# Holding back the second MoE's weight loads until the first MoE has reached a given point

## The chip, the cores and the metric

The kernel runs on one core of a Trainium2 chip. The metric is the device time in microseconds (us) of one execution. The engines are named as in the profile: PE (matrix products), PEld (its weight loads), DVE (vector), ACT (scalar), POOL (GpSimd), SP (the queue that issues nearly all DMAs).

## The reference, cut to what matters

Three stages follow one another. The first is causal attention over 4 batches, 8 heads, 576 positions and 64 values a head, mixed with a memory term. Its output, 2304 tokens of 512 values, goes through two dense "MoE" layers:

```python
h = x @ w_in                       # first MoE: 512 -> 2048
g = h * sigmoid(h)
x = g @ w_out                      # 2048 -> 512
g = x @ w_gate                     # second MoE: 512 -> 1536, two products
out = (g * sigmoid(g) * (x @ w_val)) @ w_out
```

## The kernel before, in words

**Precision.** The MoE weights arrive as 64-bit numbers. Each 128x512 tile of them is loaded raw (512 KB), turned into fp32 by one ACT and three DVE operations (`decode`, L659 to L662), and split into a high and a low part whose sum is the fp32 number; ACT makes the high part and POOL the low one. A product then takes three passes: high times high, low times high, high times low.

**First MoE.** `moe1` walks over 32 segments (a block of 256 or 320 tokens times a quarter of the 2048 hidden columns). For each of the four hidden tiles of a segment, `s1` makes the product h (PE, L784), the activation th (ACT L791, DVE L792), its high part gh (ACT L195) and its low part gl (POOL L794). So there are 128 results gl, in a fixed order; they live in 5 buffers. The second product y (PE, L842) uses them, and its partial sums go to yp (DVE L847). The weights of this stage are decoded once, written to DRAM and reloaded from there (w<-wd, L688).

**Attention** is cut into small steps ("slots") that the program emits between the pieces of the first MoE. It uses all engines: PE for transposes and products, DVE for minima and copies, ACT for exponentials, POOL for scaling (L464).

**Weights of the second MoE.** 36 raw tiles (12 groups j, three tiles each: gate, val, out) are prepared while attention and the first MoE run. The generator `prep_w2` loads a tile with `load64` (L645 or L650), decodes it, makes for each group four sums and differences S on POOL (L918 to L921), splits everything (`halves`: ACT L195, POOL L907) and stores the parts in DRAM (L892). There are three raw buffers, and the program asks for the load two tiles ahead of the decoding. `open_w2` is the end of this: it prepares groups up to 9, then gives up the memory of attention for other pools, prepares groups 10 and 11 there, transforms the first tokens of the second MoE (`y_prep`, POOL L961), and loads the output weights (`wos`, L1008).

**Second MoE.** `up` (L1046) and `down` (L1114) run after the first MoE's last segment, in an order of PE written out by hand.

**What sets the order.** The kernel is written with a framework that allocates buffers, sets all semaphores and orders the instructions of each engine before the run: the earlier an instruction stands in the program, the higher its priority, but one whose inputs and buffers are ready by the framework's own estimate may be put ahead of earlier ones that are not. On the chip each engine, and the SP queue, then runs its list in that order.

Of the kernel before, what the change touches and what calls it, by code (L numbers as in the profile page):

```python
# [8 lines left out]
F32 = mybir.dt.float32  # L9
# [12 lines left out]
    raw=2,  # L22
# [18 lines left out]
    gl='p',  # L41
# [45 lines left out]
def kernel(  # L87
# [15 lines left out]
    nc = tc.nc  # L103
# [16 lines left out]
    def f(ap):  # L120
        return ap.bitcast(F32)
# [23 lines left out]
    cur, ph2 = {"raw": rawp}, {}  # L145
# [47 lines left out]
    def cp(e, out, in_):  # L193
        if e == "a":
            nc.scalar.copy(out, in_)  # L195
        else:
            (nc.vector if e == "v" else nc.gpsimd).tensor_copy(out, in_)
# [7 lines left out]
    def tt(e):  # L205
        return nc.vector if e == "v" else nc.gpsimd
# [431 lines left out]

    w1 = {}

    def load64(w, j, part):
        raw = cur["raw"].tile([P, 512, 2], I32, tag="raw8", name="raw8", bufs=CFG["raw8"])
        w2 = w.bitcast(I32)
        if part == 0:
            nc.sync.dma_start(  # L645
                out=raw.rearrange("p (k n) t -> p k (n t)", k=KD),
                in_=w2[:, 2 * P * j:2 * P * (j + 1)].rearrange("(k p) n -> p k n", p=P),
            )
        else:
            nc.sync.dma_start(out=raw.rearrange("p n t -> p (n t)"), in_=w2[P * j:P * j + P, :])  # L650
        return raw
# [18 lines left out]
    def raw_w1(*key):  # L670
        if key in seen:
            return None
        if key[0] == 0:
            return load64(w1_in, key[1], 0)
        raw = cur["raw"].tile([P, 512, 2], I32, tag="raw8", name="raw8", bufs=CFG["raw8"])
        _, s, e = key
        nc.sync.dma_start(
            out=raw.rearrange("p (j n) t -> p j (n t)", j=NW),
            in_=w1_out.bitcast(I32)[P * NW * s:P * NW * (s + 1), 2 * P * e:2 * P * (e + 1)].rearrange(
                "(j p) n -> p j n", p=P  # L680
            ),
        )
        return raw
# [70 lines left out]
    def moe1():  # L754
        keys = []
        for n, sg in enumerate(segs):
            if n == 0 or sg["s"] != segs[n - 1]["s"]:
                keys.append(sg["s"])
        prep1.add([(0, j) for j in SLICES[keys[0]]] + [(1, keys[0], e) for e in range(KD)])
        yield ("init", 0)  # L760
        gs = [{} for _ in segs]
        fresh = [0]

        def get_x(n):
            yield ("need", ready[segs[n]["b"], segs[n]["blk"][0] // SA])

        def s1(n, ji):
            sg = segs[n]
            s, nt = sg["s"], sg["blk"][1]
            j = SLICES[s][ji]  # L770
            xh, xl = xs[sg["b"], sg["blk"][0] // SA]
            assert n_x[sg["b"], sg["blk"][0] // SA] == NP
            if ji == 0 and sg["last_use"]:
                nk = SLICES[segs[n + 1]["s"]]
                prep1.add([(0, c) for c in nk])
                fresh[0] += len(nk)
            wh, wl = prep1.need((0, j))
            wh = wh.rearrange("p (k n) -> p k n", k=KD)
            wl = wl.rearrange("p (k n) -> p k n", k=KD)
            ps = bank("h")  # L780
            m = 0
            for w, x in ((wh, xh), (wl, xh), (wh, xl)):
                for kk in range(KD):
                    nc.tensor.matmul(  # L784
                        ps[:, :nt], w[:, kk, :], x[:, kk, :nt], start=(m == 0), stop=(m == 3 * KD - 1)
                    )
                    m += 1
            th = mt.tile([P, TM], F32, tag="th", name="th", bufs=CFG["th"])
            gh = mg.tile([P, TM], F32R, tag="gh", name="gh")
            gl = mg.tile([P, TM], F32R, tag="gl", name="gl")  # L790
            nc.scalar.activation(out=th[:, :nt], in_=ps[:, :nt], func=ACTF.Tanh, scale=0.5 / WS)  # L791
            nc.vector.scalar_tensor_tensor(th[:, :nt], th[:, :nt], 1.0, ps[:, :nt], ALU.add, ALU.mult)  # L792
            cp(CFG["gh" if n >= CFG["n0"] else "gh0"], gh[:, :nt], th[:, :nt])
            tt(CFG["gl" if n >= CFG["n0"] else "gl0"]).tensor_sub(gl[:, :nt], th[:, :nt], f(gh[:, :nt]))  # L794
            gs[n][j] = (gh, gl)
            if sg["last_use"]:
                del prep1.done[(0, j)]
                if ji >= CFG["f1"] and fresh[0] > 0:
                    prep1.step()
                    fresh[0] -= 1  # L800
            elif prep1.todo or prep1.raws:
                prep1.step()
            yield ("g", 12 * nt)

        turn = [0]

        def bank(name):

            if "g" not in ph2:
                return ps_m.tile([P, 512], F32, tag="m", name=name)  # L810
            turn[0] += 1
            i = turn[0] % 8
            if i < 3:
                return ps_m.tile([P, 512], F32, tag="m", name=name)
            return sum_bank("acbdb"[i - 3], name)

        LA = CFG["la"]
        for n, sg in enumerate(segs):
            b, blk, s = sg["b"], sg["blk"], sg["s"]
            t0, nt = blk  # L820
            yield from get_x(n)
            if sg["first"]:
                yps[b, blk] = mx.tile([P, KD, TM], F32, tag="yp", name="yp", bufs=CFG["yp"])
            yp = yps[b, blk]
            for ji in range(len(gs[n]), NW):
                yield from s1(n, ji)
                if ji == CFG["xa"] and n + 1 < len(segs) and segs[n + 1]["b"] == b:
                    yield from get_x(n + 1)
            if n + 1 == len(segs):
                stream()  # L830
            if n + 1 < len(segs) and LA:
                yield from get_x(n + 1)
                for ji in range(LA):
                    yield from s1(n + 1, ji)
            for e in range(KD):
                ps = bank("y")
                m, last = 0, 3 * len(SLICES[s]) - 1
                for wi, gi in ((0, 0), (1, 0), (0, 1)):
                    for ji, j in enumerate(SLICES[s]):
                        w, g = prep1.need((1, s, e))[wi], gs[n][j][gi]  # L840
                        c = slice(P * ji, P * ji + P)
                        nc.tensor.matmul(ps[:, :nt], w[:, c], g[:, :nt], start=(m == 0), stop=(m == last))  # L842
                        m += 1
                if sg["first"]:
                    nc.scalar.mul(yp[:, e, :nt], ps[:, :nt], 0.5 / WS**2)
                else:
                    nc.vector.scalar_tensor_tensor(  # L847
                        yp[:, e, :nt], ps[:, :nt], 0.5 / WS**2, yp[:, e, :nt], ALU.mult, ALU.add
                    )
                if sg["last"]:  # L850
                    nc.sync.dma_start(
                        out=yd[P * e:P * e + P, b * S + t0:b * S + t0 + nt], in_=yp[:, e, :nt]
                    )
                if sg["last_use"]:
                    while fresh[0] > 0:
                        prep1.step()
                        fresh[0] -= 1
                    del prep1.done[(1, s, e)]
                    prep1.add([(1, segs[n + 1]["s"], e)])
                    if e >= CFG["f2"]:  # L860
                        prep1.step()
                yield ("g", 3 * len(SLICES[s]) * nt)
# [18 lines left out]
    def prep_w2():  # L881
        todo = [(j, part) for j in range(F2) for part in range(3)]
        raws, post = [], []

        def fetch(n):
            while todo and len(raws) < n and not ("hold" in ph2 and n > 1):
                j, part = todo.pop(0)
                raws.append(load64((w2_gate, w2_val, w2_out)[part], j, part // 2))

        def flush():  # L890
            for d, t in post:
# [48 lines left out]
    def sum_bank(tag, name):  # L940
        return ph2["g"].tile([P, 512], F32, tag=tag, name=name, bufs=2 if tag == "b" else 1)
# [79 lines left out]
    def stream():  # L1021

        j = len(streamed) % F2
        ws = {}
        for t, d in enumerate(wd2[j]):
            w = wp.tile([P, 2, 512], F32, tag="w", name="w")
            w = w.rearrange("p a (b c) -> p (a b) c", c=256)
            n = d.shape[1]
            nc.sync.dma_start(out=w[:, 0:n], in_=d)
            for x in range(n // 2):  # L1030
                ws[PIECES[2 * t + x]] = (r_(w[:, 2 * x]), r_(w[:, 2 * x + 1]))
        streamed.append(ws)
# [91 lines left out]
    if True:  # L1124
# [50 lines left out]
        with tc.manual_schedule(engines={mybir.EngineType.PE}):  # L1175
            for n in range(NB2 * F2):
                i, j = divmod(n, F2)
# [56 lines left out]
```

## Time and profile before

| what | value |
|---|---|
| median of 3 runs | 1163.76 us (1161.03 to 1165.37) |
| the profiled execution | 1163.68 us |
| its span, first to last instruction | 1161.9 us |
| outside the span | 1.8 us |
| busy: PE, DVE, ACT, POOL | 95%, 56%, 45%, 48% of the span |
| granted clock of PE, mean | 0.975 |

Busy time of PE is counted from modelled ends of overlapping matmuls, so a stretch in which PE is busy throughout can still differ in the matmuls that it holds. The granted clock is a share of 2.4 GHz; the lower of the two levels is 1.2 GHz, so a mean of 0.95 in a stretch means that the lower level held for a tenth of it.

### The profile page before, as it was taken

The page shows a single profiled execution, that of the slowest core. Times are in us where ns is not written, and L with a number is a line of the kernel's source. Part 1 is how long each engine was busy: PE and PEld are TensorE (multiplying, and loading weights), DVE is VectorE, ACT ScalarE, POOL GpSimd, SP SyncE. Part 2 cuts the span into 40 slices and gives each one's busy share as a digit, 9 for nine tenths or more (in the row PEclk, how much of TensorE's full clock was granted, in tenths as well). Part 3 has the DMA queues.
Part 4 walks back from the last instruction along what each step waited for, and adds up shares of the span by engine and source line. Part 5 has one row for each costly group of instructions (what it writes and reads, how often), then busy time and mean ns, then how long its engine had stood idle before and what let it go on. Part 6 is the DMA issues. An engine that isn't in the chain of part 4 may idle for free.

```text
span 1161.9 us, 19100 instructions
## 1 busy us (share of the span) xinstructions
PE 1100.5 (95%) x6803; PEld 985.9 (85%) x6803; DVE 653.2 (56%) x1413; ACT 518.1 (45%) x1237; POOL 554.6 (48%) x566
## 2 busy tenths in 40 slices
PE   7899999988989899999999799999999999999998
PEld 5576877887879788899988699899989999999986
DVE  6996777789977888425647422433353332333320
ACT  6754766456755565634645322222242223323222
POOL 4565574569887878614536922311172122312113
PEclk9989999999989899999999799999999999999999
DMA  9975755568779685544307596666665554645511
GB/s 217 295 221 158 241 182 169 172 187 271 243 246 334 219 290 189 167 151 125 108 19 278 201 413 213 219 195 196 197 235 171 156 190 150 194 154 191 160 32 55
DMA packets 155919, 226.72 MB, mean 195 GB/s; under 512 B 75696, under 2 KB 108464, under 8 KB 155824
## 3 DMA queue, kind: packets, MB, share of 16 engines
q1 hardware_dynamic: 153648, 225.10, 60.0%
q8 instruction: 54, 0.88, 0.3%
q10 hardware_dynamic: 2176, 0.40, 0.2%
q14 instruction: 41, 0.34, 0.1%
HBM read 170.93 MB, written 54.53 MB: 194 GB/s over the span
## 4 chain that ended last, share of the span: by engine, by line
PE 69%; DVE 13%; DMA 5%; POOL 5%; issue 4%; ACT 4%; SPq 0%; ACTq 0%; POOLq 0%; DVEq 0%
PE y L842 13%; PE po L1114 12%; PE h L784 11%; PE gb L1046 9%; PE ga L1046 6%; PE U L555 3%; PE gd L1046 3%; PE gc L1046 3%; PE pst L322 2%; PE pss L422 2%; DMA wo<-wo 2%; POOL s L464 2%; DVE t L661 2%; PE pss L417 1%; DVE t L662 1%
## 5 line engine op out<-in xcount | busy, mean ns | idle before, releaser
L1100 POOL TENSOR_TENSOR pl<-r,ph 128x384 fp32r<-128x384 f32 x72 | 75.1, 1052 | 315.0 <-ACT ph L1099 254.0
L784 PE MATMUL h<-xh,w 128*128 128x320 f32 (+1 forms) x1024 | 170.7, 306 | 19.6 <-DVE th L792 15.8
L842 PE MATMUL y<-gh,w 128*128 128x320 f32 (+1 forms) x1024 | 181.5, 314 | 6.7 <-DVE th L792 4.2
L794 POOL TENSOR_TENSOR gl<-th,gh 128x256 fp32r<-128x256 f32 (+1 forms) x128 | 114.4, 897 | 141.4 <-ACT gh L195 77.6
L784 PEld LDWEIGHTS h<-xh,w 128*128 128x128 f32 x1024 | 147.2, 193 | 28.2 <-DVE th L792 16.8
L842 PEld LDWEIGHTS y<-gh,w 128*128 128x128 f32 x1024 | 152.9, 199 | 20.3 <-issue 9.3
L464 POOL TENSOR_TENSOR s<-s,r 128x128 f32<-128x128 f32 (+4 forms) x144 | 118.7, 854 | 64.6 <-DVE r L481 27.1
L1114 PE MATMUL po<-wo,ph 128*128 128x512 f32 x432 | 134.0, 395 | 3.4 <-ACT ot L1120 2.2
L1046 PE MATMUL gb<-yT,w 128*128 128x384 f32 x648 | 132.0, 338 | 0.6 <-ACT gb L1070 0.6
L1046 PEld LDWEIGHTS gb<-yT,w 128*128 128x128 f32 x648 | 116.1, 188 | 10.3 <-ACT gb L1070 1.3
L792 DVE SCALAR_TENSOR_TENSOR th<-th,h 128x256 f32<-128x256 f32 (+1 forms) x128 | 57.1, 448 | 90.6 <-ACT th L791 90.3
L1073 DVE TENSOR_TENSOR gd<-gb,e 128x384 f32<-128x384 f32 x36 | 20.4, 567 | 149.7 <-PE gb L1046 149.7
L842 PE MATMUL y<-gl,w 128*128 128x320 f32 (+1 forms) x512 | 97.7, 306 | 2.5 <-POOL gl L794 2.5
L784 PE MATMUL h<-xl,w 128*128 128x320 f32 (+1 forms) x512 | 94.5, 305 | 0.0
L195 ACT CAST gh<-th 128x256 fp32r<-128x256 f32 (+1 forms) x128 | 54.7, 431 | 86.6 <-DVE th L792 47.5
L1114 PEld LDWEIGHTS po<-wo,ph 128*128 128x128 f32 x432 | 79.1, 188 | 12.3 <-ACT ot L1120 3.1
L1046 PE MATMUL ga<-yB,w 128*128 128x384 f32 x432 | 87.2, 337 | 0.0
L1114 PE MATMUL po<-wo,pl 128*128 128x512 f32 x216 | 84.5, 399 | 0.7 <-POOL pl L1100 0.7
L431 ACT ACTIVATE s<-s,mn 128x128 f32<-128x128 f32 (+3 forms) x128 | 71.3, 558 | 29.9 <-DVE mn L427 29.1
L842 PEld LDWEIGHTS y<-gl,w 128*128 128x128 f32 x512 | 79.8, 197 | 5.6 <-POOL gl L794 3.2
L784 PEld LDWEIGHTS h<-xl,w 128*128 128x128 f32 x512 | 78.2, 196 | 3.1 <-issue 2.6
L791 ACT ACTIVATE th<-h 128x256 f32<-128x256 f32 (+1 forms) x128 | 51.6, 407 | 65.0 <-PE h L784 43.5
(141 smaller groups left out, 2060.1 us busy)
## 6 DMA issues: line engine op xcount, KB each, us to landing
w<-wg SPq DMA_DIRECT2D x108, 512.0 KB, 4.2
w<-wd SPq DMA_DIRECT2D x80, 512.0 KB, 5.1
wg<-wo SPq DMA_DIRECT2D x36, 512.0 KB, 4.6
wd<-w SPq DMA_DIRECT2D x32, 512.0 KB, 4.3
raw<-in_moe_w_out_dram SPq DMA_DIRECT2D x28, 512.0 KB, 4.4
wo<-wo SPq DMA_DIRECT2D x24, 512.0 KB, 6.7
w<-wg SPq DMA_DIRECT2D x36, 256.0 KB, 3.4
raw<-in_moe_w_in_dram SPq DMA_DIRECT2D x16, 512.0 KB, 4.9
```

The lines of the kernel that those rows point to most:

```text
L195: nc.scalar.copy(out, in_)
L431: nc.scalar.activation(out=a, in_=a, func=ACTF.Exp, scale=-1.0, bias=mn, accum_out=o["sm", sup][:, col:col + 1])
L464: nc.gpsimd.tensor_mul(a, a, r.to_broadcast([P, w]))
L555: nc.tensor.matmul(U[64 * hh:64 * hh + 64, c0:c1], row_of("v", c)[:, hh], a(hh), start=False, stop=(m == len(todo) - 1), skip_group_check= ...
L784: nc.tensor.matmul(ps[:, :nt], w[:, kk, :], x[:, kk, :nt], start=(m == 0), stop=(m == 3 * KD - 1))
L791: nc.scalar.activation(out=th[:, :nt], in_=ps[:, :nt], func=ACTF.Tanh, scale=0.5 / WS)
L792: nc.vector.scalar_tensor_tensor(th[:, :nt], th[:, :nt], 1.0, ps[:, :nt], ALU.add, ALU.mult)
L794: tt(CFG["gl" if n >= CFG["n0"] else "gl0"]).tensor_sub(gl[:, :nt], th[:, :nt], f(gh[:, :nt]))
L842: nc.tensor.matmul(ps[:, :nt], w[:, c], g[:, :nt], start=(m == 0), stop=(m == last))
L1046: nc.tensor.matmul(dst, ws[nw][wi][:, P * kk:P * kk + P], y[ny][:, yi, kk], start=(start and m == 0), stop=(stop and m == 5), skip_group_c ...
L1100: nc.gpsimd.tensor_sub(pl, r, f(ph))
L1114: nc.tensor.matmul(po[t], a[:, c], w, start=(j == 0 and n == 0), stop=(j == F2 - 1 and n == 2))
```

## The change

`load64` gets an optional result `after`. Where it is given, POOL first copies one column of that result into the first column of the raw tile, and the DMA that fills the tile has to follow this write. `prep_w2` passes the newest gl that the program has emitted at that point. The loads of the first MoE's weights call `load64` without it.

```diff
-    def load64(w, j, part):
+    def load64(w, j, part, after=None):
         raw = cur["raw"].tile([P, 512, 2], I32, tag="raw8", name="raw8", bufs=CFG["raw8"])
         w2 = w.bitcast(I32)
+        if after is not None:
+            nc.gpsimd.tensor_copy(raw.bitcast(F32)[:, 0, 0:1], f(after))
         if part == 0:
             nc.sync.dma_start(
...
             gs[n][j] = (gh, gl)
+            cur["gl"] = gl[:, 0:1]
...
-                raws.append(load64((w2_gate, w2_val, w2_out)[part], j, part // 2))
+                raws.append(load64((w2_gate, w2_val, w2_out)[part], j, part // 2, cur["gl"]))
```

Walking through the loops of the program tells which gl each load gets. Numbering the gl from 1 to 128 and the raw tiles from 0 to 35: tiles 0 to 3 get gl 30; tile 4 gets 35; 5 and 6 get 38; 7 gets 42; 8 to 18 get 45, 46, 50, 52, 54, 58, 59, 62, 66, 66 and 69; 19 to 28 get 74, 74, 76, 81, 82, 83, 88, 90, 90 and 95; 29 gets 101; 30 to 34 get 102; 35 gets 107.

## Rows read from the trace of the kernel before

**Rows 1.** Windows by stretch: length, then each engine's busy us, clock, DMA share, GB/s.

```profile
120.00:240.00 120.00, 120.00 (x797) 96.42 (x794) 89.95 (x248) 72.58 (x191) 71.33 (x79) 1.00 0.60 195
240.00:330.00 90.00, 74.79 (x513) 67.86 (x514) 87.48 (x163) 59.27 (x144) 77.91 (x74) 0.94 0.76 238
330.00:480.00 150.00, 138.16 (x967) 126.68 (x967) 120.44 (x251) 87.97 (x219) 122.40 (x125) 0.95 0.76 254
480.00:611.00 131.00, 131.00 (x963) 121.19 (x963) 62.46 (x185) 61.29 (x160) 51.40 (x63) 0.99 0.32 99
611.00:670.00 59.00, 48.90 (x318) 47.23 (x315) 37.79 (x42) 26.23 (x56) 47.29 (x37) 0.86 0.70 246
670.00:740.00 70.00, 67.87 (x496) 67.44 (x495) 22.91 (x44) 18.55 (x43) 22.04 (x22) 1.00 0.71 268
740.00:1110.00 370.00, 365.81 (x1917) 340.48 (x1917) 132.16 (x207) 108.58 (x217) 82.56 (x69) 1.00 0.59 188
```

**Rows 2.** Waits of PE, 240 to 480 us: total us, times, longest.

```profile
PE h L784 <- DVE th L792: 7.7, 2, 4.1
PE pss L417 <- DVE tb L197: 6.5, 3, 4.1
```

**Rows 3.** Windows, decodes alone (L662): length, DVE busy us (count), clock, DMA.

```profile
240.00:330.00 90.00, 12.94 (x13) 0.94 0.76 238
330.00:480.00 150.00, 20.08 (x17) 0.95 0.76 254
480.00:611.00 131.00, 0.00 (x0) 0.99 0.32 99
```

**Rows 4.** Windows, gl alone (L794): length, POOL busy us (count), clock, DMA.

```profile
0.00:330.00 330.00, 37.59 (x41) 0.96 0.71 216
330.00:480.00 150.00, 25.92 (x28) 0.95 0.76 254
480.00:611.00 131.00, 22.67 (x28) 0.99 0.32 99
```

**Rows 5.** Timeline of SP and of POOL: start us, us, instruction, idle before.

```profile
444.63 0.33 SPq L650 DMA_DIRECT2D raw<-in_moe_w_out_dram  x1
...
611.67 0.38 SPq L645 DMA_DIRECT2D raw<-in_moe_w_gate_dram  x1
...
643.56 1.30 POOL L794 TENSOR_TENSOR gl<-th,gh 128x320 fp32r<-128x320 f32 x1
```

**Rows 6.** Groups of DVE, 240 to 480 us: count | busy us, mean ns | idle.

```profile
L662 DVE SCALAR_TENSOR_TENSOR t<-raw,t 128x512 int32<-128x512 int32 x30 | 33.0, 1103 | 0.3
L661 DVE SCALAR_TENSOR_TENSOR t<-raw,t 128x512 int32<-128x512 int32 x30 | 32.8, 1096 | 0.5
L660 DVE TENSOR_SCALAR t<-t 128x512 int32<-128x512 int32 x30 | 20.3, 678 | 6.0 <-ACT t L659 5.7
```

**Rows 7.** Groups of POOL, 240 to 480 us.

```profile
L907 POOL TENSOR_TENSOR wo<-t,wo 128x512 fp32r<-128x512 f32 (+1 forms) x30 | 37.6, 1256 | 11.7 <-ACT wo L195 11.5
L907 POOL TENSOR_TENSOR wo<-S,wo 128x512 fp32r<-128x512 f32 x20 | 29.7, 1492 | 4.2 <-issue 1.6 <-ACT wo L195 1.3 <-POOL wo L907 0.8
L918 POOL TENSOR_TENSOR S<-t 128x256 f32<-128x256 f32 x10 | 9.1, 913 | 2.1 <-DVE t L662 2.0
```

**Rows 8.** Single lines of the decode, whole run: duration ns min/median/max.

```profile
L662 DVE SCALAR_TENSOR_TENSOR t<-raw,t x36: 676/1102/2345, 242.7 to 653.8; 128x512 int32<-128x512 int32 x36
L661 DVE SCALAR_TENSOR_TENSOR t<-raw,t x36: 676/1102/1792, 241.4 to 652.2; 128x512 int32<-128x512 int32 x36
L660 DVE TENSOR_SCALAR t<-t x36: 410/582/2071, 241.0 to 649.3; 128x512 int32<-128x512 int32 x36
```

**Rows 9.** Single line L197 on POOL, whole run: duration ns min/median/max.

```profile
L197 POOL COPY q<-Q x32: 228/462/700, 38.1 to 573.6; 64x64 f32<-64x64 f32 x32
```

**Rows 10.** Waits of the SP queue, 223 to 460 us.

```profile
SPq L650 <- DVE t L662: 23.8, 8, 6.7
SPq L645 <- DVE t L662: 19.6, 9, 6.0
```

**Rows 11.** Timeline of SP and PE: first output-weight loads, first use.

```profile
675.32 0.80 SPq L1008 DMA_DIRECT2D wo<-wo  x2
...
746.39 0.51 PE L1114 MATMUL po<-wo,ph 128*128 128x512 f32 x1 [1.16 <-ACT ph L1099]
```

## The prediction

> **What bounds the kernel now.** I read the windows by stretch first, because the kernel has stages with different limits, then who PE waits for, then where the preparation of the second MoE's weights lies.
>
> From 740 us on, in the second MoE, PE is busy for 365.8 of 370 us at a granted clock of 1.00 [rows 1]. Nothing of the change runs there, so that part stays. From 120 to 240 us, where attention and the first MoE overlap, PE is busy throughout at clock 1.00, with DVE busy 75% and POOL 59%. Then comes the stretch to look at: from 240 to 330 us DVE is busy 97% (87.5 of 90) and POOL 87%, and PE idles 15.2 us at a clock of 0.94; from 330 to 480 us DVE is at 80%, POOL at 82%, and PE idles 11.8 us at 0.95. From 480 to 611 us PE is full again, at 0.99, and DVE is at 48%, POOL at 39%. From 611 to 670 us PE idles 10.1 us at 0.86.
>
> The longest waits of PE between 240 and 480 us are for DVE: for the activation th and for a copy of attention [rows 2]. PE has no such wait from 480 to 611 us. So DVE, slowed together with POOL, holds PE up in the first of these stretches and leaves it alone in the second.
>
> What fills DVE and POOL is seen in the counts of the decode: 13 tiles from 240 to 330 us, 17 from 330 to 480, none from 480 to 611 [rows 3]; the other 6 come after 611. So 30 of the 36 tiles are prepared as early as their buffers allow, far ahead of their place in the program.
>
> PE's loss in 240 to 480 us: 15.2 + 11.8 = 27.0 us idle, and 0.06 x 90 + 0.05 x 150 = 12.9 us by the clock, 39.9 together. With 0.01 x 131 = 1.3 in 480 to 611 us it is 41.2 over 371 us. The tail, 611 to 670 us, loses 10.1 + 0.14 x 59 = 18.4.
>
> **What the gate does.** A load now follows a gl. By 330 us 41 gl have run, by 480 us 69, by 611 us 97 [rows 4]. Against the list of gates, 7 tiles may have been loaded by 330 us (gates up to 38), 19 by 480 (up to 69), 29 by 611 (up to 95). Before it was 13, 30 and 30. The sharpest case is tile 29, loaded at 444.6 us, whose gate is gl 101, at 644 us; loads 30 to 34, which started at 611.7 us, get gl 102 [rows 5]. So the gates bite, by 33 us at the first tile and 200 at tile 29: that the change does nothing is excluded. I assume that a tile is prepared soon after its gate, as nothing else has changed for it.
>
> **The cost of a tile.** In 240 to 480 us a decode takes (33.0 + 32.8 + 20.3) / 30 = 2.87 us of DVE [rows 6]. The splits take 37.6 + 29.7 us of POOL, the sums four rows of 8.6 to 9.1 us, of which one is shown [rows 7]: with 9.1 each, 103.7 / 30 = 3.46 us of POOL a tile.
>
> **The loads after the change**, in the clock of the kernel before. 240 to 330 us: 7 tiles for 13, so DVE 87.5 - 6 x 2.87 = 70.3 (78%) and POOL 77.9 - 6 x 3.46 = 57.1 (63%). 330 to 480 us: 12 for 17, DVE 106.1 (71%), POOL 105.1 (70%). 480 to 611 us: 10 for none, DVE 62.5 + 28.7 = 91.2 (70%), POOL 51.4 + 34.6 = 86.0 (66%).
>
> **What that is worth to PE** is shown by no row directly, so I bound it. At the rate of 120 to 240 us (DVE 75%, POOL 59%: no idle, clock 1.00) the whole 41.2 us would go. At the rate of 330 to 480 us (DVE 80%, POOL 82%: 11.8 + 7.5 = 19.3 us in 150, 12.9%) the 371 us would lose 47.9, 7 more than now. The new levels lie nearer to the first row on DVE, and a third of the way to the second on POOL; and attention is of a heavier kind after 240 us than before. I take half of the upper end: 20 us gained.
>
> The decode's price is not fixed either. Alone, its three operations take 0.68 + 0.68 + 0.41 = 1.77 us at least, against the 2.87 above [rows 8]. The ten tiles moved behind 480 us would so cost DVE 17.7 to 28.7 us; I used the dearer. The Trainium skill speaks against hoping for the cheaper: "SBUF — State Buffer", section "Who interferes with whom", says that a DVE instruction with two SBUF inputs contends with a GpSimd instruction that reads SBUF, as they share a read port; L661 and L662 have two such inputs. The trace agrees in that the medians are 1.6 times the minima. By that rule a tile that still meets a two-thirds busy POOL keeps most of the 2.87, and the sum stays as it is; by the minima the gain would be up to 11 us of DVE time larger.
>
> **The 36 added copies** on POOL, one column of 128 rows, are nowhere in the trace. The nearest row is a 64x64 copy, 0.23 us at least and 0.46 in the median [rows 9]: 8 to 17 us of POOL at most. POOL's idle third covers them (45 us even in 480 to 611); without cover all 17 would count. I take 2 us.
>
> **The wait that the copies add.** A raw buffer is free when its last tile is decoded. So far SP waited for that, 43.4 us in 17 waits [rows 10], and only DMAs stood behind it. Now a POOL copy waits, and behind it in POOL's list stand gl, the scaling of attention and the low parts of the splits. It is nothing where the gate comes later than the buffer's release, and the gates come 33 to 200 us later than the old issue times, so I put it at 0 and carry the full price as a rival. On SP, the load itself now waits for POOL, with the reloads w<-wd and attention's rows behind it; those orders are set with the gate known, so 0 again, with the 6.7 us of the longest such wait as the upper end.
>
> **The tail.** Seven tiles instead of six come after 611 us. gl 102 needs five more gl after the 97th; at 131 / 28 = 4.7 us each that is some 23 us, and tile 29 has to be prepared before the memory changes hands. So the tail begins up to 35 us later. What is late next are the output weights: their loads start at 675.3 us and their first use is at 746.4 [rows 11], 71 us of slack, so the delay is hidden. If that cover were gone, the 35 us would count. The tail's own loss, 18.4 us for six tiles, is 3.1 a tile: one more costs 3 us (0 to 18).
>
> **Sum.** 1163.7 - 20 + 2 + 3 = 1148.7, so 1149 us, for an execution that lies within 0.1 us of the median. The likeliest case's own range: 41 gained and nothing paid gives 1123, 10 gained and 5 paid 1159.
>
> **Rivals.** (1) The loss only moves. 480 to 611 us has no loss now and gets ten tiles; at 12.9% it would lose 16.9 us, 15.6 more than now. With 20 gained before and 5 paid, the time is 1164; I put the case at 1158 to 1169. For it: PE is full there only while DVE is at 48%. Against: PE is just as full at 75% in 120 to 240 us.
>
> (2) POOL stands still at the copies: slower. The place is a copy put ahead of gl work in POOL's list while the decode that frees its buffer runs late; five loads share gl 102 over three buffers, four share gl 30. Fully paid, 43 us on the forecast give 1192, half gives 1170. It turns the result slower from 21 us of POOL standing that reach PE. For it: DVE operations were up to twice their usual length. Against: the late gates.
>
> (3) The tail sets the start of the second MoE. It would have to come 71 us late, and the steps above find 35; I give it no chance of its own.
>
> **Numbers.** Forecast 0.62, rival (1) 0.20, rival (2) 0.18. A measurement here tells 0.5% (5.8 us) from no change. Faster by more than that is the forecast, 0.62; within it most of (1), 0.19; slower the rest of (1) and (2), 0.19. The range 1128 to 1172 leaves out the best tenth of the forecast and the dear half of (2).
>
> **What would show it.** Right: decodes counted at about 7, 12 and 10 in the three stretches (by gl counts, if the clock shifts), DVE under 80% in each, PE's waits for DVE th mostly gone in 240 to 330 us, and the first MoE ending some 15 us earlier, with the second as long as before. Wrong: waits of POOL copies for DVE L662 of more than 20 us (rival 2); PE idle or a lower clock in 480 to 611 us (rival 1); a first use of the output weights that waits for their DMA.

## The result, and the profile after

The changed kernel takes 1149.73 us (median of 3, 1148.27 to 1150.8) against 1163.76: a ratio of 0.9881, 95% interval 0.9847 to 0.9916. The forecast was 1149. The sum met the time, but with terms that were off in both directions, so that it came within 1 us is luck. The experiments show besides that changes which gate nothing move the time by 5.6 and 9.0 us.

The windows of the changed kernel in the stretches of [rows 1], same columns:

```profile
240.00:330.00 90.00, 84.01 (x598) 80.03 (x599) 65.55 (x144) 52.85 (x131) 59.76 (x72) 0.94 0.64 210
330.00:480.00 150.00, 139.70 (x1003) 126.98 (x1002) 108.51 (x253) 88.16 (x226) 102.41 (x120) 0.97 0.58 184
480.00:611.00 131.00, 127.00 (x940) 117.69 (x939) 88.30 (x208) 70.00 (x172) 89.53 (x105) 1.00 0.63 220
611.00:670.00 59.00, 50.55 (x368) 50.05 (x367) 36.01 (x48) 27.12 (x59) 45.63 (x43) 0.97 0.76 268
670.00:740.00 70.00, 62.46 (x406) 60.91 (x406) 21.21 (x39) 17.82 (x38) 21.25 (x22) 0.93 0.79 296
740.00:1110.00 370.00, 368.36 (x1932) 343.41 (x1931) 130.27 (x206) 108.49 (x217) 82.76 (x69) 1.00 0.55 175
```

DVE has fallen from 87.48 to 65.55 us in the first stretch and risen from 62.46 to 88.30 in the third. PE idles 6.0, 10.3 and 4.0 us in the first three, where it was 15.2, 11.8 and 0 [rows 1]. The tail is worse in its second part: 7.5 us idle at a clock of 0.93 from 670 to 740 us, against 2.1 at 1.00.

The decodes alone (now L665), which answer to [rows 3]:

```profile
240.00:330.00 90.00, 6.08 (x9) 0.94 0.64 210
330.00:480.00 150.00, 9.25 (x11) 0.97 0.58 184
480.00:611.00 131.00, 8.30 (x10) 1.00 0.63 220
611.00:670.00 59.00, 6.75 (x7) 0.97 0.76 268
```

So 9, 11, 10 and 7 tiles instead of 13, 17, 0 and 6. (A tile that is at work on a boundary counts on both sides.)

The new instruction, as a single line of the source (columns as in [rows 8]), and all that POOL waited there in the whole run (total us, times, longest):

```profile
L646 POOL COPY raw<-gl x36: 173/183/709, 249.0 to 647.5; 128x1 f32<-128x1 f32 x36
```

```profile
POOL raw L646 <- DVE t L665: 0.6, 1, 0.6
```

36 copies of 0.18 us, and one wait of 0.6 us for a raw buffer. The gates hold as listed under the change: each copy comes after its gl, 34 of them by 0.1 to 8 us, those of tiles 33 and 34 by 22 and 25. The first load goes out 26 us later than before and that of tile 29 167 us later.

Waits of PE, 600 to 720 us, in the kernel before and, below the dots, in the changed one:

```profile
PE h L784 <- DVE th L792: 8.1, 2, 5.7
PE y L842 <- DMA w<-wd: 2.1, 1, 2.1
PE y L842 <- POOL gl L794: 1.7, 2, 1.4
...
PE y L846 <- DMA w<-wd: 6.2, 1, 6.2
PE h L787 <- DVE th L795: 5.5, 1, 5.5
PE h L787 <- DMA w<-wd: 2.9, 1, 2.9
```

And what stood on the SP queue ahead of the 6.2 us wait, with the product that ended it, from the timelines of SP and PE:

```profile
686.44 1.64 SPq L691 DMA_DIRECT2D w<-wd  x2
688.25 10.30 SPq L1012 DMA_DIRECT2D wo<-wo  x12
699.57 1.60 SPq L691 DMA_DIRECT2D w<-wd  x2
...
709.70 2.07 PE L846 MATMUL y<-gh,w 128*128 128x256 f32 x8 [6.24 <-DMA w<-wd]
```

Twelve output-weight loads of 512 KB went out in one row, and two reloads of first-MoE weights right behind them. The kernel before had such a row too, but earlier, with twelve reloads behind it:

```profile
675.32 10.17 SPq L1008 DMA_DIRECT2D wo<-wo  x12
686.49 27.09 SPq L688 DMA_DIRECT2D w<-wd  x12
```

Two marks of PE's timeline divide every run well: the end of the last attention product (L555), and the first product of the second MoE. All experiments are read by them. Ahead of the first mark lie 2298 to 2306 recorded products of the first MoE in every kernel, so it cuts all of them at nearly the same point of the work. What follows the second mark took 430.8 to 434.1 us, so nothing below concerns it.

| kernel | ratio to before (95%) | attention's end, us | from there to the second MoE, us |
|---|---|---|---|
| before | 1 | 611.5 | 117.8 |
| changed: tiles 0-35 gated | 0.9881 (0.9847-0.9916) | 599.7 | 116.2 |
| e1: copies from a constant, POOL | 0.9949 (0.9932-0.9966) | 608.2 | 113.3 |
| e9: copies from a constant, ACT | 0.9914 (0.9897-0.9930) | 602.8 | 112.4 |
| e10: tiles 29-35 gated | 0.9951 (0.9935-0.9968) | 608.2 | 115.4 |
| e4: tiles 0-11 gated | 0.9974 (0.9959-0.9989) | 603.5 | 118.0 |
| e8: tiles 12-35 gated | 0.9819 (0.9794-0.9844) | 599.6 | 111.6 |
| e2: 0-35 gated, column written by ACT | 0.9917 (0.9899-0.9936) | 606.3 | 113.6 |
| e5: 0-35 gated, output weights late | 0.9807 (0.9781-0.9834) | 600.8 | 109.3 |
| e3: tiles 0-28 gated | 0.9785 (0.9768-0.9802) | 596.5 | 106.0 |
| e6: 0-28 gated, output weights late | 0.9802 (0.9778-0.9827) | 598.1 | 104.5 |
| e11: tiles 12-28 gated | 0.9791 (0.9778-0.9804) | 599.3 | 108.3 |
| e12: 0-28 gated, constant for the rest | 0.9769 (0.9745-0.9793) | 598.4 | 103.4 |
| e7: no DVE decode, no gate | 0.9765 (0.9738-0.9793) | 594.1 | 111.2 |

The marks come from one profiled execution each; those of e4 and e9 were 4.4 and 5.6 us faster than their medians, so their marks lie early.

### The profile page after: what moved, and what is told of

Read it like the earlier page. It is cut to its first block, busy times and chain, and to the rows that moved or that the text cites. A ratio compares the mean times of both kernels' runs of the same rounds, so it can differ in the third digit from the quotient of the medians.

```text
span 1147.9 us, 19173 instructions
## 1 busy us (share of the span) xinstructions
PE 1089.9 (95%) x6803; PEld 979.9 (85%) x6803; DVE 636.1 (55%) x1413; ACT 517.5 (45%) x1237; POOL 551.2 (48%) x602
## 4 chain that ended last, share of the span: by engine, by line
PE 69%; DVE 11%; DMA 7%; POOL 6%; issue 3%; ACT 2%; SPq 0%; POOLq 0%; ACTq 0%; DVEq 0%
PE y L846 13%; PE po L1118 13%; PE h L787 10%; PE gb L1050 9%; PE ga L1050 6%; PE U L555 3%; PE gd L1050 3%; PE gc L1050 3%; DMA raw<-in_moe_w_val_dram 3%; PE pst L322 2%; PE pss L422 2%; POOL s L464 2%; POOL gl L797 1%; DVE t L664 1%; PE pss L417 1%
## 5 line engine op out<-in xcount | busy, mean ns | idle before, releaser
L846 PE MATMUL y<-gh,w 128*128 128x320 f32 (+1 forms) x1024 | 178.1, 310 | 9.3 <-DMA w<-wd 6.2
L787 PEld LDWEIGHTS h<-xh,w 128*128 128x128 f32 x1024 | 145.4, 191 | 24.6 <-DVE th L795 11.8
L797 POOL TENSOR_TENSOR gl<-th,gh 128x256 fp32r<-128x256 f32 (+1 forms) x128 | 111.0, 873 | 108.5 <-ACT gh L195 54.1
L1050 PEld LDWEIGHTS gb<-yT,w 128*128 128x128 f32 x648 | 116.7, 189 | 10.1 <-ACT gb L1074 1.3
L1050 PEld LDWEIGHTS ga<-yB,w 128*128 128x128 f32 x432 | 77.6, 190 | 2.1
```

The costliest lines, as they stand in the source:

```text
L787: nc.tensor.matmul(ps[:, :nt], w[:, kk, :], x[:, kk, :nt], start=(m == 0), stop=(m == 3 * KD - 1))
L1050: nc.tensor.matmul(dst, ws[nw][wi][:, P * kk:P * kk + P], y[ny][:, yi, kk], start=(start and m == 0), stop=(stop and m == 5), skip_group_c ...
```

## The experiments

**e1, the copies without the gate.**

```diff
-raws.append(load64(..., j, part // 2, cur["gl"]))
+raws.append(load64(..., j, part // 2, ident[:, 0:1]))
```

> The 36 column copies stay, but copy from a constant that exists from the start, so no load waits for a gl. Theory (the gain comes from when the tiles are prepared): the decodes lie early again, about 13, 17 and 0 in 240-330, 330-480 and 480-611 us, and the time is 1162 to 1168 us, the kernel before plus the copies. Rival A (any new order of the instruction lists brings this gain): 1148 to 1157. Rival B (POOL stands at the copies for the raw buffers, which SP did before, 43 us in all): 1172 or more.

1157.06 us. The decodes are early, as the theory wants (window of L665, 480 to 611 us, none):

```profile
240.00:330.00 90.00, 11.09 (x12) 0.89 0.66 213
330.00:480.00 150.00, 17.94 (x18) 0.99 0.77 268
480.00:611.00 131.00, 0.00 (x0) 1.00 0.33 102
```

But the time is 5.6 us below the kernel before, under the range of the theory. Rival B falls: the copies do wait for raw buffers here,

```profile
POOL raw L646 <- DVE t L665: 7.6, 5, 3.8
...
POOL raw L646 <- PE U L555: 5.1, 1, 5.1
```

yet the kernel is not slower. Rival A is partly right: copies that gate nothing bring something.

**e9, a second change without a gate.**

```diff
-nc.gpsimd.tensor_copy(raw.bitcast(F32)[:, 0, 0:1], f(after))
+nc.scalar.copy(raw.bitcast(F32)[:, 0, 0:1], f(after))
...
-raws.append(load64(..., j, part // 2, cur["gl"]))
+raws.append(load64(..., j, part // 2, ident[:, 0:1]))
```

> A second neutral change: the 36 column copies from a constant, on ACT, so again no gate. It measures how far the time moves by a new order of the lists alone (the same copies on POOL gave 0.9949). Theory (the gate gives most of the gain, the order some us either way): 1156 to 1168, attention's end between 605 and 613 us. Rival (a new order explains all of it): 1152 or less.

1154.19 us, 9.0 below the kernel before as measured along with it (1163.16), outside the theory's range by 2 us and short of the rival's. Its decodes are as early as before (14, 17 and none). So a change that gates nothing can be worth 5 to 9 us here. What differs is seen in the order of the two traces: by operation and names, the instructions of PE, DVE, ACT and POOL run in the same order in e9 and in the kernel before up to about 266 us, some 40 us behind the first load of a raw tile, and in another order from then on. Every engine's list behind a changed instruction is planned anew. That the time comes from this order is an inference: nothing else was changed, but no run takes the order alone.

**e2, the gate with the column written by ACT.**

```diff
-nc.gpsimd.tensor_copy(raw.bitcast(F32)[:, 0, 0:1], f(after))
+nc.scalar.copy(raw.bitcast(F32)[:, 0, 0:1], f(after))
```

> The column is written by ACT instead of POOL, from the same gl. Theory: the gate is what matters and the copies (36 of 0.18 us on POOL in the changed kernel) cost at most 2 us, so 1147 to 1152. Rival (the copies and the waits in front of them on POOL cost several us): 1145 or less. If ACT, in whose list the activations th stand, is hurt by waiting for POOL's gl: 1155 or more.

1153.4 us, between the bands. The decodes are spread as in the changed kernel (8, 11, 10 and 7 by their ends), and nothing is gained by freeing POOL, so the copies cost POOL nothing that reaches the end. Its ratio, 0.9917, lies above the changed kernel's 0.9881, with intervals that overlap, and the difference is no larger than what e1 and e9 show new lists to do; that ACT is hurt isn't shown. Against e9, its twin without the gate (0.9914), it wins nothing.

**e7, without the DVE work of the decode.** The kernel before, without L660 to L662 for the second MoE's tiles.

```diff
 nc.scalar.activation(out=t, in_=u, func=ACTF.Abs, scale=2.0**-111)
+if not full:            # second MoE's tiles
+    return t
 nc.vector.tensor_single_scalar(ti, ti, 3, op=ALU.logical_shift_left)
```

> The kernel before, with the three DVE operations of the decode left out for the 36 tiles of the second MoE (its weights are then not decoded), so some 86 us of DVE work are gone from 240 to 480 us; loads, ACT, POOL and stores stay early and as many. Theory (DVE's work in the crowded stretch is what held PE): attention ends 12 us earlier or more and the time is 1138 to 1150. Rival A (the early DMA traffic or POOL was it): 1157 or more. Decodes can't be counted in it.

1137.78 us, 0.2 below the theory's band, and attention's end 17.4 us earlier. The windows of this kernel:

```profile
240.00:330.00 90.00, 83.17 (x582) 75.71 (x581) 55.10 (x139) 67.45 (x169) 79.35 (x90) 0.96 0.87 276
330.00:480.00 150.00, 144.70 (x1019) 132.33 (x1018) 76.84 (x199) 88.77 (x217) 105.48 (x118) 0.98 0.72 242
```

POOL is as busy as before in the first stretch (79.35 us), the DMA engines busier (0.87), and PE idles 6.8 us instead of 15.2. So the DMA traffic and POOL's load in themselves were not what held PE there; DVE's work was. From 330 to 480 us POOL is at 105 us instead of 122, so there the two are not told apart. 17.4 us is twice what new lists without a gate gave (8.7, e9).

**e4 and e8, gates on a part.**

```diff
-cur["gl"]
+cur["gl"] if j < 4 else None      # e4;  e8: j >= 4
```

> Only tiles 0 to 11 are gated, 12 to 35 load as buffers come free. Theory (what counts is how much DVE and POOL work is crowded into one stretch): the first stretch is relieved, the other tiles crowd behind tile 11 between about 370 and 500 us with DVE over 80% there, and about half of the gain is left, 1152 to 1160. Rival (only the first 90 us, with DVE at 97%, were a loss): as the full change, 1147 to 1151.

1159.91 us for e4. The theory's crowd behind tile 11 is there: 18 decodes from 330 to 480 us, DVE at 128.13 of 150, PE idle 16.3:

```profile
330.00:480.00 150.00, 133.72 (x920) 120.28 (x918) 128.13 (x265) 91.57 (x227) 125.17 (x127) 0.95 0.75 244
```

> Only tiles 12 to 35 are gated; 0 to 11 load early. Theory: 240 to 330 us stays crowded (DVE over 93%, PE idle some 15 us there), 330 to 480 is relieved, the tail is that of the full change: 1152 to 1158. Rival (only how late the tiles come as a whole counts, not the first stretch): 1147 to 1151.

1144.24 us for e8, which is the rival's side and lower still. Its first stretch stays crowded; the second is nearly free:

```profile
240.00:330.00 90.00, 79.45 (x548) 72.36 (x548) 83.87 (x160) 60.23 (x148) 77.66 (x75) 0.94 0.73 227
330.00:480.00 150.00, 146.71 (x1072) 136.48 (x1071) 91.94 (x236) 81.54 (x210) 87.98 (x105) 0.98 0.53 169
```

PE idles 10.6 and 3.3 us, 13.8 together, where the changed kernel has 16.3, and 6.1 from 480 to 611 us, where that has 4.0. Attention ends at 599.6 us, as with all gates. So relieving the first 90 us is not needed: what is lost there is won from 330 to 480 us, where 7 tiles are decoded instead of 11. That what counts is how much of this work is left for after 480 us, where DVE had room, fits e4 and e8, but no run varies that alone.

**e3, the tail free.**

```diff
-cur["gl"]
+cur["gl"] if 3 * j + part < 29 else None
```

> Only tiles 0 to 28 are gated; 29 to 35 load as soon as a buffer is free. Theory (the tail's gate costs about one tile, 3 us): 1145 to 1149, the loads after the change of memory start at attention's end and not some 17 us later. Rival (the late tail pushes the output-weight loads in front of the first MoE's last reloads, for which PE waits 9 us in the changed kernel): 1140 or less. If the tail's gate is itself of use, because it keeps POOL free for gl: 1152 or more.

1138.21 us, 11.5 below the changed kernel, past the theory's band and in the rival's. PE's waits from 600 to 720 us are now 3.7 for th and 1.1 for reloads:

```profile
PE h L787 <- DVE th L795: 3.0, 1, 3.0
PE y L846 <- DMA w<-wd: 1.1, 2, 0.6
PE y L846 <- DVE th L795: 0.7, 1, 0.7
```

**e5 and e6, the output weights late.**

```diff
 for j in range(F2):                       # open_w2
     wos[j] = ph2["wo"].tile(...)
-    nc.sync.dma_start(out=wos[j], in_=wdo[j])
+    if j < 2:
+        nc.sync.dma_start(out=wos[j], in_=wdo[j])
...
 up(i, j, units)                           # second MoE
+if i == 0 and j + 2 < F2:
+    nc.gpsimd.tensor_copy(r_(wos[j + 2][:, 0, 0:1]), pt[0, 0, j][:, 0:1])
+    nc.sync.dma_start(out=wos[j + 2], in_=wdo[j + 2])
```

> The changed kernel, but of the twelve output-weight loads only two are issued before the second MoE; each of the others follows a result of it, two steps ahead of its use. Theory 1 (in the tail PE waits 9.1 us for reloads of first-MoE weights, because the twelve loads stand in front of them on the queue): these waits go and the time is 1138 to 1144 us. Theory 2 (the gated tail is long for another reason, POOL and DVE work that comes late): 1147 us or more.

1142.38 us: theory 1. Of the waits for reloads the one of 6.2 us is gone, the other is nearly as long as it was (2.5 us), and the stretch behind attention is 6.9 us shorter. Waits of PE, and the queue around the last reloads:

```profile
PE h L787 <- DVE th L795: 7.0, 1, 7.0
PE h L787 <- DMA w<-wd: 2.5, 1, 2.5
...
689.44 1.64 SPq L691 DMA_DIRECT2D w<-wd  x2
691.25 0.79 SPq L1013 DMA_DIRECT2D wo<-wo  x2
692.09 1.62 SPq L691 DMA_DIRECT2D w<-wd  x2
```

> Gates on tiles 0 to 28 alone, and the output-weight loads late. With the free tail PE waits only 1.1 us for reloads, so both theories say 1135 to 1140 us, at most 2 us better than the free tail alone; more than 5 us better or worse would say that the order of the tail matters in a way that neither has.

1140.51 us, no better than e3, half a microsecond above the band: without the wait nothing is won.

**e10, e11 and e12, the tail once more.** e10 gates tiles 29 to 35 alone, e11 tiles 12 to 28 alone; e12 is e3 with a copy from the constant for tiles 29 to 35.

```diff
-cur["gl"]
+cur["gl"] if 3 * j + part >= 29 else None               # e10
+cur["gl"] if 12 <= 3 * j + part < 29 else None          # e11
+cur["gl"] if 3 * j + part < 29 else ident[:, 0:1]       # e12
```

> Only tiles 29 to 35 are gated. Theory (the early gates give the gain, the tail's gate costs up to 10 us): attention ends at 607 to 613 us as in the kernel before, and the time is 1160 to 1172. Rival (the tail's gate is harmless, and the free tail was short by the luck of its order): 1152 to 1160.

1156.78 us: the rival's band. Attention ends at 608.2 us as forecast, so the early gates are missing; but the tail is no longer than the kernel before's. A late tail alone does not cost 10 us. (Up to 450 us this kernel's lists are those of the kernel before.)

> Gates on tiles 12 to 28 alone: the first twelve early, the tail free. Attention ended at the same time with and without gates on the first twelve (599.7 and 599.6 us), and the free tail was 10 us shorter, so: 1135 to 1141, as with gates on 0 to 28. If the gates on the first twelve are of use after all: 1143 or more.

1138.74 us, as expected: tiles 0 to 11 need no gate. Its second stretch is as free as that of e8:

```profile
330.00:480.00 150.00, 147.15 (x1083) 136.93 (x1082) 92.24 (x237) 82.38 (x211) 87.75 (x105) 0.99 0.52 169
```

> As the free tail (gates on tiles 0 to 28), but the seven tail tiles get a column copy from a constant: no gate, and another order of the tail's lists. From the end of attention to the start of the second MoE it took 106.0, 104.5 and 108.3 us in three kernels with early gates and a free tail, 109.3 to 116.2 in five with a gated tail. Theory (a free tail behind gated tiles is short by itself): 1136 to 1142 us, 103 to 109 us for that stretch. Rival (the order's luck made it short): 112 us or more, and a time of 1145 or more.

1136.32 us, as expected, with other lists in the tail: the short tail of e3 was not one order's luck. e12 has the lowest time of the kernels that do the whole computation, 27 us below the kernel before as measured along with it (1163.48). That e3, e11 and e12 differ from one another isn't shown; their intervals overlap.

## Why the prediction was right, point by point

**DVE holds PE up in the crowded stretch: shown.** e7 takes DVE's decode away and leaves the loads, and attention ends 17.4 us earlier. The sign named for it came too: from 240 to 330 us PE waited 9.1 us for th before, 7.7 of them for the product h [rows 2], and in the changed kernel only 2.3, with a wait of attention beside it:

```profile
PE pss L417 <- DVE Kl L378: 3.6, 1, 3.6
PE h L787 <- DVE th L795: 2.3, 1, 2.3
```

**The loads after the change: right.** Forecast 7, 12, 10 and 7 tiles, measured 9, 11, 10 and 7. DVE was to be at 78, 71 and 70%; it is at 73, 72 and 67% (65.55, 108.51, 88.30 us). POOL: 63, 70, 66% against 66, 68, 68%.

**The price of a tile: between the ends.** The decode from 240 to 611 us in the changed kernel, groups of DVE:

```profile
L664 DVE SCALAR_TENSOR_TENSOR t<-raw,t 128x512 int32<-128x512 int32 x29 | 27.3, 941 | 0.5
...
L665 DVE SCALAR_TENSOR_TENSOR t<-raw,t 128x512 int32<-128x512 int32 x29 | 23.6, 815 | 0.3
...
L663 DVE TENSOR_SCALAR t<-t 128x512 int32<-128x512 int32 x29 | 19.9, 688 | 12.9 <-ACT t L662 12.9
```

70.8 / 29 = 2.44 us, where I kept 2.87 and the operations alone took 1.77. So a part of the gain may be work that got shorter: 29 x 0.43 = 12 us of DVE. All of it lies on the two operations with two inputs (mean 1096 and 1103 ns before [rows 6], 941 and 815 now); the third took 678 and takes 688.

The trace of the kernel before shows what POOL has to do with it. Two instructions of L661 there, the first while POOL does nothing until 420.88 us, the second beside a busy POOL:

```profile
418.55 0.68 DVE L661 SCALAR_TENSOR_TENSOR t<-raw,t 128x512 int32<-128x512 int32 x1
420.88 0.73 POOL L794 TENSOR_TENSOR gl<-th,gh 128x256 fp32r<-128x256 f32 x1 [3.53 <-ACT gh L195]
...
304.35 3.16 POOL L907 TENSOR_TENSOR wo<-S,wo 128x512 fp32r<-128x512 f32 x2
304.71 1.67 DVE L661 SCALAR_TENSOR_TENSOR t<-raw,t 128x512 int32<-128x512 int32 x1
```

Of the 72 instructions of L661 and L662 for the second MoE's tiles, the 15 that met no POOL instruction all took 676 to 693 ns; the 37 that had POOL beside them throughout took 1311 ns in the mean. The Trainium skill's rule on the port shared by DVE and GpSimd ("SBUF — State Buffer", "Who interferes with whom") names such instructions with two SBUF inputs, and the trace agrees. But L660, with one input, behaves alike (410 to 428 ns for the 11 without POOL, 888 in the mean for the 22 with it), so of the 0.67 us that the changed kernel pays above 1.77, 0.28 lie on an operation that I had not counted under that rule.

**The gain on PE: the mis-sized term.** I took 20 us, half of 41.2. The same reading of the changed kernel gives idle 6.0 + 10.3 + 4.0 and by the clock 0.06 x 90 + 0.03 x 150 = 9.9, 30.2 together: 11.0 regained. Attention's end says the same, 611.5 to 599.7, 11.8 us. Rival (1) was right in part: 480 to 611 us, where nothing was lost by waiting, now idles 4.0 us. And the clock did not recover in the first stretch, 0.94 as before. The step of the sum that was mis-sized is this one: half of the upper end, where a quarter came. By stretches, 9.2 us came back in the first, 4.5 in the second, and 2.7 were lost in the third; in the second PE's idle time fell by only 1.5 us, though DVE went from 80 to 72% and POOL from 82 to 68%.

**The copies: 2 us taken, nothing found.** Their 36 x 0.18 = 6.6 us and the 0.6 us of waiting are hidden on POOL; e2 moves them off it and wins nothing. Rival (2) does not occur, for the reason given against it: the gates come later than the buffers. In e1, where the copies do wait for buffers (12.7 us in the two rows shown), the kernel is not slower either.

**The tail: +3 us taken, -1.6 measured, and for another reason than I gave.** The span from attention's end to the second MoE went from 117.8 to 116.2 us, in which three things nearly cancel: less waiting for th and gl (9.8 us before, 5.5 after), more for reloads (2.1 before, 9.1 after), and a higher clock (0.93 before, 0.96 after, by which some 4 us less are lost). The delay of up to 35 us did not come: in the changed kernel gl 102 is done at 616.5 us, and the loads behind the change of memory start 5 us later than before, the last three 20 to 26. I looked at whether the output weights would arrive in time, and they do; I missed that their row of loads, 13 us later than before, while the second MoE starts 13.5 us earlier, now stands in front of the last reloads. e5 shows it: with ten of those loads out of the way the stretch is 6.9 us shorter.

**The sum.** -11.8 - 1.6 - 0.5 behind the second mark = -13.9, the difference of the spans (1161.9 and 1147.9) but for rounding, against -20 + 2 + 3 = -15. The gain was over-estimated by 8 us, and the costs by 7. The mechanism was right, the two sizes were not, and that they cancel was luck.

**How much of it is the gate.** Two changes without a gate gave 5.6 and 9.0 us. Of the pairs that differ in the gate alone, the one on POOL says that it is worth 7 us (0.9881 against e1's 0.9949, intervals apart), the one on ACT that it is worth nothing (e2's 0.9917 against e9's 0.9914). So for a gate on all 36 tiles, the change that I forecast, I can't split the 14 us, and a good part of them may be new lists; all three neighbours without an early gate (e1, e9, e10) are faster than the kernel before.

For the early gates as such the evidence is better, as it holds over many lists. The time with gates on at least tiles 12 to 28 (changed, e2, e3, e5, e6, e8, e11, e12) is 0.9769 to 0.9917 of that before, and 0.9914 to 1 with no early gate (before, e1, e9, e10); only e2 and e9 meet. (e4, which gates tiles 0 to 11 alone, is in neither group: 0.9974.) Attention's end is 599.8 us on average over the first group (596.5 to 606.3) and 607.7 over the second (602.8 to 611.5). So the early gates are worth about 8 us there, with about 4 us either way from the lists. And PE's idle time follows the place of the decodes through all these lists:

| gates on tiles | 240-330 us: tiles decoded, PE idle us | 330-480 us | 480-611 us |
|---|---|---|---|
| none early (before, e1, e9, e10) | 12-13, 14.0-16.6 | 16-18, 10.0-11.8 | 0, 0-0.1 |
| 0 to 28 or more (changed, e2, e3, e5, e6, e12) | 8-9, 6.0-10.3 | 10-11, 9.7-10.5 | 10-11, 3.7-6.2 |
| 12 to 28 or more (e8, e11) | 12, 10.6-10.7 | 7, 2.9-3.3 | 10-11, 5.6-6.1 |

**What stays open.** Why the tail is short only when it is free and stands behind gated tiles (103.4 to 108.3 us in e3, e6, e11 and e12), and not when nothing is gated (112.4 to 117.8 in before, e1 and e9) or when only the first twelve are (118.0 in e4). e10 excludes the tail's gate as the whole cause; e12 excludes one particular order. What is short is known: from the first mark to the second PE idles 12.2 us at a clock of 0.93 before, 14.7 at 0.96 in the changed kernel, and 3.1 at 0.98 in e12. The windows of e12 show the first part of it:

```profile
611.00:670.00 59.00, 57.06 (x420) 56.63 (x420) 29.77 (x52) 27.75 (x64) 50.62 (x48) 0.97 0.84 306
```

DVE works 29.77 us in a stretch where it worked 37.79 before [rows 1], at a POOL load that is no lower. Why it comes so was not tried.

## What to carry to other kernels

Where a planner fills gaps with work that is needed much later, count that work by stretch: an engine at 80 to 97% in two stretches and at 48% in the next says that holding it back is worth trying, and the utilisation that results could be worked out well beforehand. The gain on the engine that matters could not: the lost time of the crowded stretches is its upper end, and here about a quarter of it came back. Before giving credit to a mechanism, run the same edit with its effect taken out (here a copy from a constant), since two such edits moved this kernel by 0.5 and 0.9%, and do it for each form of the edit, as the pairs on POOL and on ACT disagree; and gate only what lies on the way, for each delayed load asks again what stands behind it on its queue.

## What the runs showed of the hardware that I had not expected

A POOL copy of one column of 128 rows takes 0.18 us in the median and 0.17 at least, less than the 0.23 of the nearest row that I had [rows 9]. A row of twelve 512 KB loads ahead of two reloads held them back by some 10 us at their issue: they follow the pair of reloads before them (686.44 us) by 13.1 us, where e5, with two loads between, has 2.7 (689.44 and 692.09). Then the product that needs them started at 709.70 us, 8.5 to 10.1 us after they were issued, where such a reload lands 5.1 us after its issue in the median of the kernel before. And the DVE operations of the decode take 0.68, 0.68 and 0.41 us where POOL does nothing, and 1.26, 1.38 and 0.89 in the mean where it works throughout.
